# An attention and gated feed-forward kernel on one core: VectorE's order in the second segment, constants, masks and the last tile

## The chip, the core and the metric

The kernel runs on one core of a Trainium2 chip. A core has TensorE (PE in the profile) for matrix products, VectorE (DVE), ScalarE (ACT) and GpSimd (POOL) for elementwise work, SyncE (SP), which here only issues transfers, and 16 DMA engines. PE writes to PSUM; VectorE and ScalarE read it from there. Each engine works through its own instructions in the order in which they stand, and waits at one whose inputs are not ready. The metric is the time of one execution in device microseconds, lower is better; three executions are shown, and one more was taken with the profiler.

## The reference

With B=4 batches, H=8 heads, S=768 positions, D=64, 4 sink positions and a window of 128:

```python
scores = scale * np.matmul(q, k.transpose(0, 1, 3, 2))
keep = is_sink | in_window              # k < 4, or 0 <= q - k < 128
scores = np.where(keep, scores, -1000000000.0)
a = np.exp(scores - max)
a = a / (np.sum(a, axis=-1, keepdims=True) + 1e-09)
x = np.matmul(a, v)                     # heads side by side: 3072 x 512
H = np.maximum(x @ w_h, 0.0)
T = 1.0 / (1.0 + np.exp(-(x @ w_t + b_t)))
out = T * H + (1.0 - T) * x
```

## The kernel before, in words

The 3072 tokens are 24 tiles of 128, six to a batch. A loop over n (L447) is a pipeline by hand: step n computes the scores and the exponential of tile n, the attention values and the division of tile n-1 (n1), and the feed-forward part of tile n-2 (nb). A helper at the end keeps each engine's instructions in the order in which the program writes them, so the order of the code is the order of each engine.

*q and k.* Each is loaded by four transfers per segment, one for each head of a group (load_part, L104); batch 0 has three segments of 256 positions, the others two of 384, called (1,0), (1,1) and so on. Most go through POOL's queue, which turns fp32 into fp16 on the way. Only the first two segments of q of batch 0 come in fp32 through SP (and half of the first through ACT) and are cast on VectorE and ScalarE, half each (cast_q, L423). VectorE then transposes in pieces of four positions per row (transpose_qk, L125): two pieces for a segment of batch 0, three for the others. All the pieces of a segment are needed before the scores that read it.

*Scores and masks.* For a tile, PE adds a mask to PSUM by eight small matmuls of mk and mq (L265; four at the last tile of a batch), then the products of k and q (L272). ScalarE takes the exponential (E, L319), 128x2048. A column of ones beside V gives the row sums. The sink positions go through sink_scores (L285), sink_expo (L293) and the vs tile (L309); vs comes from the sinks' V and a mask vmask, multiplied on POOL (sink_values, L254). sink_scores for batch 1 stands first in step n=8 and reads all of that batch's q, so it needs both its segments.

*Values and the feed-forward part.* values (L330, L333) multiplies E by V; norm (L341, L343, VectorE) divides and gives X. X is transposed on PE (L354) and copied to XT on ScalarE (L359). gate (L363) adds the product with wt to the bias row in ps_z (L303), tanh follows on ScalarE (L370); hidden (L379) puts the product with wh into ps_h, of which there is one. VectorE then makes diff (L386), gate_value (L374, on POOL for tiles 14 to 22), gated (L391); POOL adds X (finish, L397; on VectorE for the last two tiles) and SP stores. I call gate_value, gated and finish of a tile its "complete". diff frees ps_h for the next hidden.

*Order in steps 2 to 7.* hidden_at (L421) says which hidden runs in which step: none in 2, tile 0 in 3, tile 1 in 4, tiles 2 and 3 in 5, then nb. pieces (L408) puts three transposes of segment (1,0) in n=5, one of (1,1) in n=6 and two in n=7, behind norm and the V cast; up to n=7 the completes come after them. cast_v (L142) is on VectorE for tiles 0 to 4, then on POOL. V tiles 2 to 7 are requested on SP behind the scores of tiles 0 to 5.

*The start.* idle (L405) is products of zeros that keep PE busy: 18 before step 0, 8 in it, 6 in step 1. SP issues the first q, the four sink loads (L173), the second q, then V. POOL issues k, the bias, the third segment, wt, wh, makes vmask (L235 to L240, nine operations), vs, and then issues (1,0). A POOL transfer waits until the eighth transfer before it on its queue has landed. VectorE sets constants by memset: ones (L222), the ones columns of eight V tiles and of the sinks (L231, L232).

Of the kernel before, what the change touches and what calls it, by code (L numbers as in the profile page):

```python
# [37 lines left out]
def kernel(  # L38
# [34 lines left out]
    LATER = 14  # L73

# [83 lines left out]
    vmask = const.tile([P, H], FP32, tag="vmask")  # L158
    skmask = const.tile([P, HG, H], FP16, tag="skmask")
# [11 lines left out]
    def load_sinks(b):  # L171
        for g in range(G):
# [5 lines left out]
              allow_small_or_imprecise_dtypes=True)  # L178
    for i in range(2):
        for g in range(G):  # L180
            load_part(0, i, g, 1)
    load_sinks(0)
    for g in range(G):
        load_part(0, 1, g, 0, into=first[1], engine=sp)
    pool.dma_start(out=brow[0:P:32, :], in_=moe_b_t.unsqueeze(0).to_broadcast([G, DM]))
# [3 lines left out]
    pool.dma_start(out=wh, in_=moe_w_h.rearrange("(kc p) of -> p kc of", p=P))  # L189
# [29 lines left out]
    def bias_row():  # L219
        dve.memset(ones, 0.0)  # L220
        for g in range(G):
            dve.memset(ones[32 * g:32 * g + 1, :], 1.0)  # L222

    def ones_columns():
        dve.memset(skmask, 0.0)
        for g in range(G):
            for hg in range(HG):
                h = hg * G + g
                dve.memset(skmask[32 * g:32 * g + 32, hg, h:h + 1], 1.0)
        for tile_v in vt:  # L230
            dve.memset(tile_v[:, :, D:D + 1], 1.0)  # L231
        dve.memset(vs32[:, :, D:D + 1], 1.0)  # L232

    def sink_masks():
        pool.memset(vmask, 1.0)  # L235
        for g in range(G):
            m = vmask[32 * g:32 * g + 32, :]
            pool.affine_select(out=m, in_=m, compare_op=ALU.is_ge, fill=0.0, base=0,
                               pattern=[[-NSINK, H]], channel_multiplier=1)
            pool.affine_select(out=m, in_=m, compare_op=ALU.is_ge, fill=0.0,  # L240
                               base=NSINK - 1, pattern=[[NSINK, H]], channel_multiplier=-1)

# [15 lines left out]
    def scores(n):  # L258
# [3 lines left out]
        for x in range(nq):  # L262
# [5 lines left out]
        for hg in range(HG):  # L268
            for e in range(2):
                for g in range(G):  # L270
# [4 lines left out]
                                     start=False, stop=(e == 1), skip_group_check=True)  # L275
# [39 lines left out]
    def expo(n):  # L315
# [4 lines left out]
                       func=AF.Exp, bias=ebias, scale=SCALE)  # L320

# [55 lines left out]
    def hidden(n):  # L377
        for kc in range(KC):
            pe.matmul(ps_h, lhsT=XT[n][:, kc * P:(kc + 1) * P], rhs=wh[:, kc, :],  # L379
                      start=(kc == 0), stop=(kc == KC - 1))  # L380
# [3 lines left out]
    def diff(n):  # L384
        DD[n] = work.tile([P, DM], FP16, tag="DD", name="DD")
        dve.scalar_tensor_tensor(out=DD[n], in0=ps_h, scalar=0.0,  # L386
                                 in1=X[n].rearrange("p hg g d -> p (hg g d)"),
                                 op0=ALU.max, op1=ALU.subtract)

    def gated(n):  # L390
        dve.tensor_tensor(out=DD[n], in0=DD[n], in1=TH[n], op=ALU.mult)  # L391

    def finish(n):

        o = work.tile([P, DM], FP32, tag="O", name="O")
        eng = dve if n >= N - 2 else pool
        eng.tensor_tensor(out=o, in0=DD[n], in1=X[n].rearrange("p hg g d -> p (hg g d)"),  # L397
                          op=ALU.add)
        sp.dma_start(out=out[n * P:(n + 1) * P, :], in_=o)


# [7 lines left out]
    for n, what in zip([5, 5, 5, 6, 7, 7, 9, 10, 11, 12, 13, 13, 15, 16, 17, 18, 19, 19],  # L409
                       [(b, i, piece) for b in range(1, B) for i in range(2) for piece in range(3)]):  # L410
# [9 lines left out]

    hidden_at = {2: [], 3: [0], 4: [1], 5: [2, 3]}  # L421

    def cast_q(i):  # L423
        dve.tensor_copy(out=nat[0][i][:, 0, 0], in_=first[i][:, 0, 0])
        act.copy(out=nat[0][i][:, 0, 1], in_=first[i][:, 0, 1])

    load_v(0)
    load_v(1)
    cast_q(0)
    transpose_qk(0, 0, 0)  # L430
    transpose_qk(0, 0, 1)
    ones_columns()
    cast_q(1)
# [4 lines left out]
    bias_row()  # L438
    sink_masks()
    sink_values(0)  # L440
    load_segment(1, 0)
    sinks_at = {2: (0, (2, 3)), 4: (0, (4, 5))}
    for b in range(1, B):
        sinks_at[b * NC + 2] = (b, (2, 3, 4, 5))

    idle(18)
    for n in range(N + 2):  # L447

        nb, n1 = n - 2, n - 1
        late = n >= N  # L450
        early = n < 8
        if nb >= 0 and not late:
# [6 lines left out]
        if n < N:  # L459
# [5 lines left out]
            if n % NC == 3 and n // NC + 1 < B:  # L465
                load_sinks(n // NC + 1)
        starts(n1 if 0 <= n1 < N else None, nb if nb >= 0 else None)
        old = hidden_at.get(n - 1, [n - 3])[-1:]
        new = hidden_at.get(n, [nb] if nb >= 0 else [])
        if nb >= 1:  # L470
            for m in old:
                diff(m)
# [4 lines left out]
        if not early:  # L477
            for piece in pieces.get(n, ()):
                transpose_qk(*piece)
        if n == 0:  # L480
            idle(8)
        if 0 <= n1 < N:
            values(n1)
            norm(n1)
        if 0 < n < LATE:
            cast_v(n, dve)
        if n == 1:
            idle(6)
        if early:
            turn = pieces.get(n, ())  # L490
            for piece in turn[:1]:
                transpose_qk(*piece)
            for m in new[:-1]:
                hidden(m)
                diff(m)
            for piece in turn[1:]:
                transpose_qk(*piece)
        if nb >= 1:
            for m in old + new[:-1]:
                if m < LATER:  # L500
                    gate_value(m)
                gated(m)
                finish(m)
        if nb >= 0:
# [5 lines left out]
            for m in new[-1:]:  # L510
                hidden(m)
# [4 lines left out]
        if n < N and n > NC and n % NC == 1:  # L516
            sink_values(n // NC)
    gate_value(N - 1)
    diff(N - 1)
    gated(N - 1)  # L520
# [36 lines left out]
```

## Time and profile before

| | us |
|---|---|
| three executions | 116.92, 118.16, 118.45 (median 118.16) |
| the profiled execution | 116.57 |
| its span, first to last instruction | 114.9 |
| busy: PE, DVE, ACT, POOL | 101.2, 83.6, 74.5, 86.0 |
| mean granted clock of TensorE | 0.975 |

The page divides the span into 40 slices and gives, for each engine, the busy tenths. "Chain that ended last" is followed back from the last instruction, each time to what released it. In a timeline a line has the start, the time taken, engine, line of the program, operation and tiles, and in brackets the idle time before it with what ended it. A DMA issue is listed with the time from its start to the landing. Busy time of PE is modelled and overlaps from one matmul to the next.

### The profile page before, as it was taken

To read this page: it belongs to the slowest core of one execution; us is meant where nothing else is said; L and a number is where in the kernel's file an instruction comes from. 1 tells how busy PE (TensorE), PEld (TensorE's weight loads), DVE (VectorE), ACT (ScalarE), POOL (GpSimd) and SP (SyncE) were. 2 spreads that over 40 slices of the span, in tenths; PEclk is the share of its full clock that TensorE was granted. 3 is DMA by queue.
4 is the path that set the end of the run, shared out by engine and by line. 5 is a ranking of instruction groups with operands and counts; after the bars stand their busy time and mean duration, and the time that the engine had idled before them with its cause. 6 is when DMAs were issued, how large, how long until landed. Compare 5 with 4: busy or idle time off the path is not lost.

```text
span 114.9 us, 3575 instructions
## 1 busy us (share of the span) xinstructions
PE 101.2 (88%) x1416; PEld 55.3 (48%) x1416; DVE 83.6 (73%) x186; ACT 74.5 (65%) x81; POOL 86.0 (75%) x143
## 2 busy tenths in 40 slices
PE   5998299999968896999999999999999999989910
PEld 2333145555535434656555565655655665544400
DVE  6772977463699997799988959898889446646570
ACT  3401766969724793997758978896678987862400
POOL 6998379859773899999997989948755986555600
PEclk9999859999999999999999999999999999999995
DMA  2999999999999399999999999997766201222222
GB/s 79 207 189 231 216 207 194 226 213 233 218 238 196 128 210 271 256 209 261 214 206 234 279 212 257 200 162 195 208 169 178 102 31 66 91 97 91 87 96 94
DMA packets 35921, 20.82 MB, mean 181 GB/s; under 512 B 27196, under 2 KB 32320, under 8 KB 35904
## 3 DMA queue, kind: packets, MB, share of 16 engines
q1 hardware_dynamic: 29536, 13.50, 44.4%
q0 software_dynamic: 6208, 6.82, 37.6%
q10 hardware_dynamic: 160, 0.26, 0.8%
q8 instruction: 11, 0.18, 0.7%
q14 instruction: 6, 0.05, 0.2%
HBM read 21.11 MB, written 6.29 MB: 239 GB/s over the span
## 4 chain that ended last, share of the span: by engine, by line
PE 46%; DVE 17%; DMA 16%; POOL 11%; issue 4%; ACT 2%; POOLq 1%; DVEq 0%; ACTq 0%
DMA nat<-in_k_dram 11%; PE ps_z L363 11%; PE ps_h L379 10%; DVE tr L125 7%; POOL nat L108 6%; PE ps_s L272 5%; DMA nat<-in_q_dram 5%; PE ps_av L330 5%; PE ps_av L333 4%; PE ps_s L265 3%; PE ps_av L354 3%; DVE X L343 3%; DVE DD L386 3%; PE ps_z L303 2%; DVE DD L391 2%
## 5 line engine op out<-in xcount | busy, mean ns | idle before, releaser
L319 ACT ACTIVATE E<-ps_s,ebias 128x2048 f16<-128x2048 f32 (+1 forms) x24 | 43.8, 1826 | 5.1 <-PE ps_s L272 4.8
L397 POOL TENSOR_TENSOR O<-DD,X 128x512 f32<-128x512 f16 x22 | 25.5, 1159 | 15.6 <-DVE DD L391 12.5
L379 PE MATMUL ps_h<-wh,XT 128*128 128x512 f16 x96 | 24.6, 379 | 1.3 <-DVE DD L386 1.3
L125 DVE STREAM_TRANSPOSE tr<-nat 128x512 f32<-128x512 f32 x24 | 24.9, 1081 | 1.0 <-DMA nat<-in_k_dram 0.8
L363 PE MATMUL ps_z<-wt,XT 128*128 128x512 f16 x96 | 24.6, 379 | 0.2 <-DMA wt<-in_moe_w_t_dram 0.2
L108 POOL DMA_DIRECT2D nat<-in_k_dram x36 | 19.7, 554 | 2.3 <-DMA nat<-in_k_dram 1.1
L386 DVE SCALAR_TENSOR_TENSOR DD<-ps_h,X 128x512 f16<-128x512 f32 x24 | 16.5, 687 | 4.5 <-PE ps_h L379 3.6
L370 ACT ACTIVATE TH<-ps_z 128x512 f16<-128x512 f32 x24 | 14.2, 592 | 7.9 <-PE ps_z L363 7.8
L359 ACT COPY XT<-ps_av 128x512 f16<-128x512 f16 x24 | 14.0, 584 | 7.8 <-PE ps_av L354 6.2
L343 DVE TENSOR_TENSOR X<-ps_av,rec 128x512 f16<-128x512 f32 x24 | 16.6, 692 | 0.9
L341 DVE RECIPROCAL rec<-ps_av 128x8 f32<-128x8 f32 x24 | 4.9, 202 | 16.3 <-PE ps_av L333 15.0
L108 POOL DMA_DIRECT2D nat<-in_q_dram x28 | 15.7, 559 | 1.1 <-DMA nat<-in_k_dram 0.5
L379 PEld LDWEIGHTS <-XT 128*128 128x128 f16 x96 | 9.2, 98 | 12.2 <-issue 1.8
L272 PE MATMUL ps_s<-tr 32*128 32x256 f16 (+1 forms) x384 | 14.5, 267 | 0.6 <-DVE tr L125 0.3
L333 PE MATMUL ps_av<-v,E 128*128 128x65 f16 x192 | 14.3, 196 | 0.0
L330 PE MATMUL ps_av<-v,E 128*128 128x65 f16 x160 | 12.5, 194 | 0.0
L333 PEld LDWEIGHTS <-E 128*128 128x128 f16 x192 | 11.8, 99 | 1.4 <-ACT XT L359 1.0
L330 PEld LDWEIGHTS <-E 128*128 128x128 f16 x160 | 10.1, 97 | 4.7 <-issue 4.7
L391 DVE TENSOR_TENSOR DD<-DD,TH 128x512 f16<-128x512 f16 x24 | 11.5, 480 | 0.7
L405 PE MATMUL ps_h<-zeros 128*128 128x512 f16 x32 | 10.7, 502 | 1.3 <-DVE zeros L175 1.3
L265 PE MATMUL ps_s<-mq,mk 32*128 32x256 bf16 x176 | 9.3, 279 | 2.7 <-ACT E L319 2.7
L142 POOL CAST v<-V 128x512 f16<-128x512 f32 x19 | 11.7, 615 | 0.0
(58 smaller groups left out, 100.5 us busy)
## 6 DMA issues: line engine op xcount, KB each, us to landing
V<-in_v_dram SPq DMA_DIRECT2D x24, 256.0 KB, 6.2
out_dram<-O SPq DMA_DIRECT2D x24, 256.0 KB, 3.3
nat<-in_q_dram POOLq DMA_DIRECT2D x24, 96.0 KB, 5.7
nat<-in_k_dram POOLq DMA_DIRECT2D x24, 96.0 KB, 5.5
first<-in_q_dram SPq DMA_DIRECT2D x6, 128.0 KB, 3.9
nat<-in_k_dram POOLq DMA_DIRECT2D x12, 64.0 KB, 4.3
wt<-in_moe_w_t_dram POOLq DMA_DIRECT2D x1, 512.0 KB, 7.3
wh<-in_moe_w_h_dram POOLq DMA_DIRECT2D x1, 512.0 KB, 8.6
```

The source lines that it names most:

```text
L108: engine.dma_start(out=into[32 * g:32 * g + 32, which].rearrange("p hg m d -> p hg (m d)"), in_=(q, k)[which][b, :, t0:t0 + nt, :].rearran ...
L125: dve.transpose(out=dst[:, :, 4 * piece:4 * piece + 4, :], in_=src)
L272: last = pe.matmul(ps_s[:, g, hg, 0:nq * P], lhsT=tr[b][rows, 1, hg, c * P:(c + 1) * P, e], rhs=tr[b][rows, 0, hg, c * P:(c + nq) * P, e], ...
L319: act.activation(out=E[n][:, :, :, 0:nq * P], in_=ps_s[:, :, :, 0:nq * P], func=AF.Exp, bias=ebias, scale=SCALE)
L330: pe.matmul(slot, lhsT=E[n - 1][:, g, hg, P:2 * P], rhs=v_of(n - 1)[:, h, :], start=first, stop=False, skip_group_check=True)
L333: pe.matmul(slot, lhsT=E[n][:, g, hg, 0:P], rhs=v_of(n)[:, h, :], start=first, stop=True, skip_group_check=True)
L343: dve.tensor_tensor(out=X[n], in0=av[:, :, :, 0:D], in1=rec.unsqueeze(3).to_broadcast([P, HG, G, D]), op=ALU.mult)
L363: pe.matmul(ps_z, lhsT=XT[n][:, kc * P:(kc + 1) * P], rhs=wt[:, kc, :], start=False, stop=(kc == KC - 1), skip_group_check=True)
L370: act.activation(out=TH[n], in_=ps_z, func=AF.Tanh, scale=0.5)
L379: pe.matmul(ps_h, lhsT=XT[n][:, kc * P:(kc + 1) * P], rhs=wh[:, kc, :], start=(kc == 0), stop=(kc == KC - 1))
L386: dve.scalar_tensor_tensor(out=DD[n], in0=ps_h, scalar=0.0, in1=X[n].rearrange("p hg g d -> p (hg g d)"), op0=ALU.max, op1=ALU.subtract)
L397: eng.tensor_tensor(out=o, in0=DD[n], in1=X[n].rearrange("p hg g d -> p (hg g d)"), op=ALU.add)
```

## The change

It has five parts.

1. The second segment of q of batch 0 is issued on SP straight behind the first; V of tiles 0 and 1 next, the sink loads last. Its cast is done by VectorE alone, 128x1024.
2. The rows of ones, the ones columns of V and of the sinks are written by 13 small ScalarE activations (Copy with bias 1). vmask starts from an iota on POOL and is finished by five small VectorE operations behind the cast of V tile 0. On POOL vs now stands ahead of wh and of segment (1,0).
3. VectorE's order in steps 4 to 8 is written out (turns). The transposes of batch 1 are spread over steps 4 to 7. In steps 0 to 3, norm comes ahead of them as before, but in step 1 the third segment's transposes now come ahead of the cast of V tile 1. idle in step 1 goes from 6 to 4.
4. For tiles 20 to 23 no mask is added on PE; VectorE multiplies E by wmask (0 or 1, made on POOL in step 15) ahead of values.
5. The last tile's hidden, diff, gated, finish and store go in two halves of 256 columns, the left finish on POOL. Tile 22's finish moves to POOL.

```diff
+    DVE_MASK = N - 4
     for i in range(2):
         for g in range(G):
             load_part(0, i, g, 1)
-    load_sinks(0)
     for g in range(G):
         load_part(0, 1, g, 0, into=first[1], engine=sp)
+    load_v(0)
+    load_v(1)
+    load_sinks(0)
...
         for tile_v in vt:
-            dve.memset(tile_v[:, :, D:D + 1], 1.0)
+            act.activation(out=tile_v[:, :, D:D + 1], in_=zeros[:, 0:H].unsqueeze(2),
+                           func=AF.Copy, bias=1.0)
...
+    def windows():
+        pool.memset(wmask, 1.0)
+        pool.affine_select(out=wmask[:, 0], in_=wmask[:, 0], compare_op=ALU.is_ge, fill=0.0,
+                           base=0, pattern=[[1, P]], channel_multiplier=-1)
...
+    def mask(n):
+        nq = 2 if n % NC + 1 < NC else 1
+        e = E[n].rearrange("p g hg (x q) -> p (g hg) x q", x=2)[:, :, 0:nq]
+        dve.tensor_tensor(out=e, in0=e, in1=wmask[:, 0:nq].unsqueeze(1)
+                          .to_broadcast([P, H, nq, P]), op=ALU.mult)
...
-    hidden_at = {2: [], 3: [0], 4: [1], 5: [2, 3]}
+    def complete(m):
+        if m < LATER:
+            gate_value(m)
+        gated(m)
+        finish(m)
+    turns = {4: [(diff, 0), (norm, 3), (transpose_qk, 1, 0, 0), (complete, 0)],
+             5: [(diff, 1), (transpose_qk, 1, 0, 1), (norm, 4), (hidden, 2), (diff, 2),
+                 (transpose_qk, 1, 0, 2), (complete, 1)],
+             6: [(diff, 3), (norm, 5), (transpose_qk, 1, 1, 0), (complete, 2)],
+             7: [(diff, 4), (transpose_qk, 1, 1, 1), (norm, 6), (transpose_qk, 1, 1, 2),
+                 (complete, 3)],
+             8: [(diff, 5), (norm, 7), (complete, 4), (complete, 5)]}
+    last_hidden = {2: (), 3: (0,), 4: (1,), 5: (3,)}
+    sink_values(0)
+    pool.dma_start(out=wh, in_=moe_w_h.rearrange("(kc p) of -> p kc of", p=P))
+    load_segment(1, 0)
...
+        if DVE_MASK <= n1 < N:
+            mask(n1)
         starts(n1 if 0 <= n1 < N else None, nb if nb >= 0 else None)
...
-            idle(6)
+            idle(4)
...
+    left, right = slice(0, DM // 2), slice(DM // 2, DM)
     gate_value(N - 1)
-    diff(N - 1)
-    gated(N - 1)
-    finish(N - 1)
+    diff(N - 1, left)
+    gated(N - 1, left)
+    finish(N - 1, left)
+    diff(N - 1, right)
+    gated(N - 1, right)
+    finish(N - 1, right, dve)
```

137 lines of the change are left out of this document (70 added, 67 removed).

## The prediction, made before the changed kernel had run

> **What bounds the kernel now.** I read the slices of the page, then the chain that ended last, then the timelines of the engines, where brackets hold the idle time before an instruction and its releaser.
>
> ```profile
> PE   5998299999968896999999999999999999989910
> DVE  6772977463699997799988959898889446646570
> ...
> PEclk9999859999999999999999999999999999999995
> DMA  2999999999999399999999999997766201222222
> ...
> PE 46%; DVE 17%; DMA 16%; POOL 11%; issue 4%; ACT 2%; POOLq 1%; DVEq 0%; ACTq 0%
> ```
>
> A slice is 2.87 us. TensorE is full from about 48 us to 105; there a tile takes 3.65 us (transposes of X at 51.79 and 55.43 in the PE timeline). Before that it has holes, with VectorE at 9 in the twelfth to fifteenth slice (31.6 to 43 us). The DMA engines are full from 2.9 us. The chain agrees: POOL and DMA to 32 us, VectorE to 44, PE to about 103, VectorE at the end. So three stretches can give something: the front, the PE-bound stretch, the tail. The front, on VectorE and TensorE:
>
> ```profile
> 28.06 0.69 DVE L343 TENSOR_TENSOR X<-ps_av,rec 128x512 f16<-128x512 f32 x1
> ...
> 31.41 0.21 DVE L341 RECIPROCAL rec<-ps_av 128x8 f32<-128x8 f32 x1 [1.07 <-ACT E L319]
> ...
> 36.55 1.28 DVE L391 TENSOR_TENSOR DD<-DD,TH 128x512 f16<-128x512 f16 x1
> ...
> 42.21 1.97 DVE L125 STREAM_TRANSPOSE tr<-nat 128x512 f32<-128x512 f32 x2
> ```
>
> ```profile
> 44.23 0.43 PE L285 MATMUL ps_av<-tr,sk 128*32 128x64 f16 x31 [0.83 <-DVE tr L125]
> ```
>
> From the end of X for tile 3 (28.75) VectorE works, idle once for 1.07, to 44.18, and the sink scores of n=8 wait for its last transpose. It is VectorE's order and not a late load that holds this: by the DMA issues, segment (1,0)'s last part was issued at 23.33 and took 5.5 (landed 28.8), (1,1)'s at 29.09 and took 5.2 (34.3), while their first transposes start at 32.26 and 39.19.
>
> The clock, in a table of 1 us stretches (PE, PEld, DVE, ACT, POOL busy with counts, PEclk, DMA share, GB/s), and the tail:
>
> ```profile
> 12.00:13.00 1.00, 0.00 (x0) 0.00 (x0) 1.00 (x2) 1.00 (x1) 0.24 (x1) 1.00 1.30 212
> ...
> 14.00:15.00 1.00, 1.00 (x24) 0.60 (x16) 0.79 (x6) 0.00 (x0) 0.55 (x1) 0.50 1.34 233
> ```
>
> ```profile
> 109.38 0.29 DVE L374 TENSOR_SCALAR TH<-TH 128x512 f16<-128x512 f16 x1
> 109.59 0.68 DVE L386 SCALAR_TENSOR_TENSOR DD<-ps_h,X 128x512 f16<-128x512 f32 x1
> 110.31 0.42 DVE L391 TENSOR_TENSOR DD<-DD,TH 128x512 f16<-128x512 f16 x1
> 110.77 0.69 DVE L397 TENSOR_TENSOR O<-DD,X 128x512 f32<-128x512 f16 x1
> ```
>
> PE waits 2.8 us (10.95 to 13.73) for E of tile 0, which waits on ScalarE behind the cast of the second q; then the clock is 0.50 for 3.3 us. At the end 2.1 us of VectorE and 3.4 us of store (111.46 to 114.9) follow the last tanh.
>
> **The front, step by step.** *Loads.* On SP the four sink loads (1.70 to 4.71) no longer stand ahead of the second q: it is issued from 1.70 instead of 4.75, V of tiles 0 and 1 somewhat earlier, the sinks behind them, needed only by vs. On POOL the nine vmask operations go (15.19 to 17.39); one iota comes (0.23, as away's), and vs now waits for VectorE's masks, at about 14 to 15, with wh and segment (1,0) queued behind it: wh at about 16 instead of 14.45, (1,0) from about 17 instead of 18.48. That buys and costs nearly nothing: landings on POOL's queue were 17.1 (last third-segment part, 11.23 + 5.9), 20.1 (wt, 12.76 + 7.3), 23.05 (wh, 14.45 + 8.6), 28.8, 34.3: in order, spaced by size (3 us per 512 KB, 5.5 to 5.8 per 768 KB) and not by issue, so the queue is always full. wh is late only if issued after wt has landed. What helps is the DMA share of 0.50 in the first 4 us, partly filled by the earlier q: everything behind lands 0 to 1.0 us earlier, or 0.5 later (V of tiles 3 and 4 is asked for earlier, as its scores are). I take 0.4 earlier.
>
> *ScalarE.* Its cast of the second q (0.62, after 5.38 of waiting) goes, so E of tile 0 starts after its scores (9.2) and not at 11.72. Thirteen small activations come: at most 0.36 each (es, 64x128), at least 0.06 (the memsets that they replace), at 0.2 done by 8.4, at 0.36 by 10.5. They lie beside the wait for the transposes: nothing; if that cover goes, 1.3 at most, still under the old 11.72.
>
> *VectorE.* Nine memsets of 0.065 and four of 0.165 go (1.2); half a cast more (0.27), the mask's five small operations between 0.06 (memset) and 0.23 (away) each come, 0.7 in all: equal within 0.3, behind loads. But third-segment transposes now stand before the cast of V tile 1: they wait for 17.1 less 0.4 and end at 18.7, the cast at 19.1 (before 17.08), values of tile 1 at 19.15 (before 19.26). So n=2 gains nothing: wt's gate at 19.7 (20.11), n=3 at 20.7 (21.02), n=4 at 24.6 (24.94): 0.3.
>
> *The five steps.* Before, X(3) to the last transpose is 15.4 us, with six transposes, three norms, diffs 1 to 4 and completes 0 to 3 in it. After, complete(3) stands behind the last transpose (0.65 out of the chain), and gated(2), 1.28 instead of 0.42 at 36.55 because POOL had started O(1) at 36.40, no longer follows complete(1) directly (0.86). Completes 4 and 5 now stand together, so gated(5) may stretch in the same way, beside PE work of n=8. Bottom-up: six transposes of 0.95, three norms of 0.9, four diffs of 0.62, three completes of 0.65, a V cast of 0.37 are 13.2; waits for values of tiles 4 and 5, about 1.0. That is 14.2, against 15.4: 1.2. The first transpose now wants (1,0) at 28.4, its landing (28.8 less 0.4): no stall, but no slack; each us later is a us in the chain, and the V cast of tile 4 and diff(1) queue behind it, for which values(4) and hidden(2) wait. (1,1) lands at 34, wanted at 37.
>
> Front: 0.3 + 1.2 + 0.1 (idle 6 to 4, hidden) = 1.6 earlier at n=8; bounds 2.3 earlier (landings 1.0 earlier) and 0.3 later (first rival). From n=8 on PE is the bound with unchanged work to n=19.
>
> **The masks.** Removed: 28 PE mask matmuls, 0.33 per eight in the chain, 0.12 for four: 1.1. Added: three multiplications of 128x2048 f16 and one of 128x1024. The f16 TENSOR_TENSOR rows are 0.194 at 64 elements and 0.42 at 512: 0.51 ns each, so 1.2 and 0.7 us. Upper bound by the f32 row (0.691 at 512): 2.4. VectorE then has 1.2 + 0.62 + 0.9 + 0.42 = 3.15 per tile, under PE's 3.32. values(n1) waits for the mask and diff queues behind it. E is ready in time: E(20) at 92.0, gated(17) ends at 92.44. POOL builds wmask at n=15 (about 0.9 by ident's two rows of 0.29), beside 1.84 of idle before 77.86; without that it would be 0.9 on the V casts. Whether VectorE and POOL run freely is doubtful:
>
> ```profile
> 91.77 0.67 DVE L391 TENSOR_TENSOR DD<-DD,TH 128x512 f16<-128x512 f16 x1
> ```
>
> ```profile
> 91.54 0.61 POOL L142 CAST v<-V 128x512 f16<-128x512 f32 x1
> ```
>
> This gated took 0.67 and ended 0.29 after POOL's cast; so did those at 36.55 and 47.91. The other 21 took about 0.42. Bounds: 1.3 gained (1.1 and its share behind norm), 0.4 lost (second rival). As most rows are free, I take 0.8 gained.
>
> **The last tile.** GV 0.29, two diffs of 0.42, two gated of 0.29, one O of 0.42 make 2.1, as before: halves add an overhead each. finish(22) moves to POOL, but gate_value waited for tanh (109.35) anyway: nothing. Left: the last store is half as large. Of its 3.4 us between nothing and 0.7 goes (256 KB at the 200 GB/s of the front are 1.3); against it the right gated may meet POOL's left O, 0.3. I take 0.4 gained.
>
> Sum: 1.6 + 0.8 + 0.4 = 2.8. The profiled execution took 116.57 (span 114.9 and 1.7 around it): 113.8. The runs were 116.92, 118.16, 118.45; the median of all four is 117.54, so I state **114.7**.
>
> **Rivals.** *The clock halves in n=2* (17%). Scores(2) end at 16.3 to 17.2, values(1) start at 19.15: a hole of 1.9 to 2.8 us. A hole of 2.8 halved the clock for 3.3 us; holes up to 0.9 did not. Then 1.6 us of work doubles in n=2 and 3, n=8 is 0.3 late: 117.54 + 0.3 - 0.8 - 0.4 = 116.6. The Trainium skill, "TensorE: Matmul & The Clock Gate", section "What's actually happening", says that the clock falls after an idle window of about 3.4 us; by that, the clock would stay and the sum hold, but this trace fell after 2.8.
>
> *POOL and VectorE take turns* (18%). If each mask and gated excludes POOL's O (1.15), gate value (0.6) and cast (0.6), a tile takes 2.35 + 0.3 + 1.2 = 3.85 instead of 3.65; three tiles lose 0.6, the first 0.33 stays, the right gated loses 0.3: 117.54 - 1.6 + 0.3 - 0.1 = 116.1. For it: the three rows above; against it: the other 21. The Trainium skill, "SBUF — State Buffer", section "SBUF: two separate sides", states it as a rule: a VectorE operation with two SBUF inputs and a GpSimd operation lock a shared port for the whole instruction, whichever starts first; it speaks against the masks, and the three rows agree.
>
> *Masks at one element per 1.1 ns* (8%), by the f32 row, because wmask is broadcast over heads: 2.4 + 2.65 = 5.05 per tile, 1.4 more on three, 0.7 on the last: 4.6 lost, 117.54 - 1.6 + 4.6 - 0.4 = 120.1, slower than before. It decides from masks of 1.7 us on (3 x (1.7 + 2.65 - 3.65) = 2.1, the rest of the gain). Against it: the two inner dimensions are contiguous.
>
> **Numbers.** Forecast 50%, rivals 17, 18, 8, and 7% that loads land earlier still and the masks are free: 116.57 - 2.3 - 1.3 - 0.7 = 112.3. The range 112.3 to 117.3 reaches past both middle rivals (a run as high as 118.16 adds 0.6) and leaves out the third and the edges. Two per cent is about what a measurement of this kernel tells from no change: 115.8 and 120.5. Faster: 47 of the forecast's 50, the 7, 6 of the middle rivals: 60%. Slower: 8 and 1. Within: 31.
>
> **What would show it.** The first L285 of n=8 near 42.6; idle on VectorE before the first transpose of segment (1,0) means a late load; PEclk 0.5 near 20 us the first rival. Mask rows near 1.2 us and tile steps of 3.3 to 3.5 from n=20 on the forecast; mask or gated rows longer beside POOL rows the second. The prediction is wrong if wh's landing stops hidden(0) or steps from n=9 to 19 are not 3.65.

## The result, and the profile after

The kernel after takes 123.69 us (median of 122.28, 123.53, 123.85 and 124.34), the kernel before beside it 117.72: a ratio of 1.047, 95% interval 1.034 to 1.060. It is slower; 114.7 was forecast. A run over 1.5% above its kernel's fastest is left out of the ratios: here the 124.34, all but one of `sinks_first`, which so has no ratio, 8 of 12 of `early_q` (118.8 to 119.8) and 5 of 12 of `order_vector_end`, whose profile, like that of `sinks_first`, is of such a run. The profiled execution took 122.28 with a span of 120.6, against 116.57 and 114.9: 5.7 us more.

The slices and the shares of the chain, on the page of the kernel after (a slice is 3.0 us):

```profile
PE   5942998999389979969999999999999999899100
...
DVE  6708967352597995999898958987794988874800
...
PEclk9999599999999999999999999999999999999855
DMA  3999999999979699999999999867843122122220
...
PE 41%; DMA 22%; DVE 17%; POOL 8%; issue 3%; ACT 3%; DVEq 0%; ACTq 0%; POOLq 0%
```

Three places to look at: PE has a 3 in the eleventh slice (30.2 to 33.2 us) and a 6 in the eighteenth (51.3 to 54.3), where before had a 9 in the slices of the same number; the chain has 22% DMA, where it had 16%; and PE and VectorE are empty in the last two slices, when the arithmetic is over and the kernel still runs. The front in VectorE's timeline, with the idle time before each instruction in brackets:

```profile
28.47 0.69 DVE L366 TENSOR_TENSOR X<-ps_av,rec 128x512 f16<-128x512 f32 x1
31.37 1.06 DVE L126 STREAM_TRANSPOSE tr<-nat 128x512 f32<-128x512 f32 x1 [2.20 <-DMA nat<-in_q_dram]
...
37.46 0.42 DVE L420 TENSOR_TENSOR DD<-DD,TH 128x512 f16<-128x512 f16 x1
...
44.18 1.06 DVE L126 STREAM_TRANSPOSE tr<-nat 128x512 f32<-128x512 f32 x1
```

gated(2) takes 0.42 as forecast (1.28 before), but the first transpose of (1,0) starts only when the load has landed, after 2.20 of idling. Steps n=8 to n=10 on PE, then the stretch of VectorE and GpSimd that holds n=10 (each line has its engine):

```profile
45.29 0.43 PE L302 MATMUL ps_av<-tr,sk 128*32 128x64 f16 x31 [0.79 <-DVE tr L126]
...
54.14 0.40 PE L377 MATMUL ps_av<-ident,X 128*128 128x128 f16 x4 [0.73 <-DVE X L366]
```

```profile
48.92 0.42 DVE L420 TENSOR_TENSOR DD<-DD,TH 128x512 f16<-128x512 f16 x1
...
49.58 2.15 DVE L420 TENSOR_TENSOR DD<-DD,TH 128x512 f16<-128x512 f16 x1
...
50.27 1.16 POOL L426 TENSOR_TENSOR O<-DD,X 128x512 f32<-128x512 f16 x1
```

The first DVE line is gated(4), the second gated(5), which took 2.15. At the end, GpSimd's and VectorE's last operations (the span ends at 120.6):

```profile
113.18 0.67 POOL L426 TENSOR_TENSOR O<-DD,X 128x256 f32<-128x256 f16 x1 [0.94 <-POOL O L426]
...
114.03 0.42 DVE L426 TENSOR_TENSOR O<-DD,X 128x256 f32<-128x256 f16 x1
```

The transposes of X of tile 8 (n=10) and of tile 23 on PE, in the kernel before, and of tile 23 in the kernel after:

```profile
51.79 0.39 PE L354 MATMUL ps_av<-ident,X 128*128 128x128 f16 x4
...
106.11 0.40 PE L354 MATMUL ps_av<-ident,X 128*128 128x128 f16 x4 [0.23 <-DVE X L343]
```

```profile
108.45 0.40 PE L377 MATMUL ps_av<-ident,X 128*128 128x128 f16 x4 [0.23 <-DVE X L366]
```

Milestones, from these lines and those of before, say where the 5.7 us went:

| stretch | before | after | lost |
|---|---|---|---|
| start to n=8 (its sink scores) | 44.23 | 45.29 | 1.06 |
| n=8 to n=10 (X transposes) | 7.56 | 8.85 | 1.29 |
| n=10 to X transposes of tile 23 | 54.32 | 54.31 | 0 |
| from there to the end of the last O | 5.35 | 6.00 | 0.65 |
| last O to the end of the span | 3.44 | 6.15 | 2.71 |

The masks on VectorE lie in the third stretch, and changed nothing.

### The profile page after: what moved, and what is told of

The parts are those of the page before. It is cut to its first block, busy times and chain, and to the rows that moved or that the text cites. A ratio compares the mean times of both kernels' runs of the same rounds, so it can differ in the third digit from the quotient of the medians.

```text
span 120.6 us, 3527 instructions
## 1 busy us (share of the span) xinstructions
PE 100.2 (83%) x1390; PEld 54.7 (45%) x1390; DVE 87.5 (73%) x183; ACT 76.2 (63%) x93; POOL 90.1 (75%) x140
## 4 chain that ended last, share of the span: by engine, by line
PE 41%; DMA 22%; DVE 17%; POOL 8%; issue 3%; ACT 3%; DVEq 0%; ACTq 0%; POOLq 0%
PE ps_z L386 9%; PE ps_h L402 9%; DMA nat<-in_k_dram 8%; DMA nat<-in_q_dram 8%; DVE tr L126 7%; DMA wh<-in_moe_w_h_dram 6%; POOL nat L109 5%; PE ps_av L353 4%; DVE X L366 4%; PE ps_s L288 4%; PE ps_av L377 4%; PE ps_av L356 3%; DVE DD L415 2%; PE ps_s L281 2%; PE ps_z L320 2%
## 5 line engine op out<-in xcount | busy, mean ns | idle before, releaser
L426 POOL TENSOR_TENSOR O<-DD,X 128x512 f32<-128x512 f16 (+1 forms) x24 | 30.4, 1269 | 13.2 <-DVE DD L420 8.8
L402 PE MATMUL ps_h<-wh,XT 128*128 128x512 f16 (+1 forms) x100 | 24.6, 370 | 0.7 <-DVE DD L415 0.7
L393 ACT ACTIVATE TH<-ps_z 128x512 f16<-128x512 f32 x24 | 14.2, 593 | 10.8 <-PE ps_z L386 10.8
L415 DVE SCALAR_TENSOR_TENSOR DD<-ps_h,X 128x512 f16<-128x512 f32 (+1 forms) x25 | 16.6, 664 | 3.3 <-PE ps_h L402 2.7
L402 PEld LDWEIGHTS <-XT 128*128 128x128 f16 x100 | 9.7, 97 | 11.8 <-issue 1.5
L364 DVE RECIPROCAL rec<-ps_av 128x8 f32<-128x8 f32 x24 | 4.7, 197 | 13.9 <-PE ps_av L356 13.9
L420 DVE TENSOR_TENSOR DD<-DD,TH 128x512 f16<-128x512 f16 (+1 forms) x25 | 12.9, 515 | 0.7
L288 PEld LDWEIGHTS <-tr 32*128 32x128 f16 x384 | 9.2, 93 | 5.3 <-DVE tr L126 4.2
L432 PE MATMUL ps_h<-zeros 128*128 128x512 f16 x30 | 10.0, 500 | 1.3 <-DVE zeros L178 1.3
```

The costliest lines, as they stand in the source:

```text
L288: last = pe.matmul(ps_s[:, g, hg, 0:nq * P], lhsT=tr[b][rows, 1, hg, c * P:(c + 1) * P, e], rhs=tr[b][rows, 0, hg, c * P:(c + nq) * P, e], ...
L393: act.activation(out=TH[n], in_=ps_z, func=AF.Tanh, scale=0.5)
L402: pe.matmul(ps_h[:, cols], lhsT=XT[n][:, kc * P:(kc + 1) * P], rhs=wh[:, kc, cols], start=(kc == 0), stop=(kc == KC - 1), skip_group_check ...
L415: dve.scalar_tensor_tensor(out=DD[n][:, cols], in0=ps_h[:, cols] if h is None else h, scalar=0.0, in1=flat(X[n], cols), op0=ALU.max, op1=A ...
L426: eng.tensor_tensor(out=O[n][:, cols], in0=DD[n][:, cols], in1=flat(X[n], cols), op=ALU.add)
```

## The experiments

Each was timed beside the kernel before. In the table, "n=8" is the start of those of its sink scores that wait for VectorE's last transpose (31 of 32), "to n=10" from there to the X transposes of n=10, "end" from the X transposes of tile 23 to the end of the span, each from one profile; "landing" is the issue of the eighth part of (1,0) plus its time to landing, good to 0.1 us. The last two kernels load and use only half of the weights and so compute something else; they stand for the timing alone.

| run | ratio (95%) | landing | n=8 | to n=10 | end |
|---|---|---|---|---|---|
| before | 1 | 28.8 | 44.23 | 7.56 | 8.79 |
| after | 1.047 (1.034-1.060) | 31.1 | 45.29 | 8.85 | 12.15 |
| whole_tile | 1.042 (1.035-1.049) | 32.5 | 47.59 | 8.84 | 10.47 |
| sinks_first | none | 30.8 | 45.86 | 8.84 | 12.09 |
| completes_apart | 1.044 (1.038-1.051) | 30.4 | 44.44 | 8.01 | 12.15 |
| pe_masks | 1.050 (1.042-1.057) | 31.2 | 45.32 | 8.84 | 12.03 |
| wh_first | 1.055 (1.048-1.062) | 31.6 | 45.69 | 8.85 | 12.15 |
| old_loads | 1.041 (1.035-1.048) | 30.3 | 44.42 | 8.86 | 12.11 |
| halves_only | 1.032 (1.023-1.040) | 31.0 | 45.51 | 7.55 | 11.71 |
| order_alone | 1.031 (1.024-1.037) | 30.8 | 44.93 | 8.02 | 10.13 |
| late_copy | 1.027 (1.021-1.032) | 29.4 | 43.98 | 7.55 | 11.96 |
| pool_early | 0.999 (0.994-1.003) | 29.8 | 44.47 | 7.56 | 8.54 |
| halves_vector | 1.003 (0.999-1.006) | 29.2 | 44.07 | 7.55 | 9.16 |
| spread_early | 1.001 (0.997-1.005) | 30.2 | 44.70 | 7.55 | 8.54 |
| vector_end | 1.032 (1.027-1.037) | 31.6 | 45.66 | 8.86 | 8.87 |
| o4_vector | 1.038 (1.032-1.045) | 31.3 | 46.39 | 7.85 | 12.07 |
| early_q | 0.998 (0.994-1.002) | 30.6 | 44.29 | 7.55 | 8.74 |
| order_vector_end | 0.999 (0.994-1.003) | 32.5 | 47.65 | 8.02 | 8.30 |
| order_half_weights | 0.987 (0.983-0.991) | 27.1 | 42.45 | 8.02 | 8.29 |
| before_half_weights | 0.991 (0.988-0.995) | 28.0 | 43.07 | 7.55 | 8.77 |

### The end

Theory first: the halves lengthen the end. Rival: something else does.

```diff
-            if n == N + 1:
-                for cols in (slice(0, DM // 2), slice(DM // 2, DM)):
-                    hidden(nb, cols)
...
-    diff(N - 1, left)
...
-    finish(N - 1, right, dve)
+    diff(N - 1)
+    gated(N - 1)
+    finish(N - 1, eng=dve)
```

> The kernel after, with only the last tile whole again (one hidden, one diff, one gated, one O on VectorE, one store of 256 KB). Theory: the halves are what makes the end long. Then the time from the last O to the end of the span is about 3.4 us as before the change, not 6.15, and the last O ends 0 to 0.6 earlier; the time falls by 2.7 to 3.3 us, to a ratio of 1.020 to 1.025 against the kernel before. Rival: the long end has nothing to do with the halves; then about 6 us stay after the last O, and the ratio is 1.042 or more.

The end fell from 12.15 to 10.47, and 4.75 stayed after the last O, where before has 3.44. So the theory had half of it: the halves are not all. The ratio stayed at 1.042, the rival's value: in this profile n=8 came at 47.59, 2.3 us later than in the kernel after, which is more than the 1.7 that the end gave back. The same from the other side, the kernel before with halves:

> The kernel before, with only the last tile in halves (two hidden, two diffs, two gated, the left O on GpSimd and the right on VectorE, two stores of 128 KB; O of the tile ahead of it on GpSimd too). Theory: the halves lengthen the end: from the last O to the end of the span 6.1 us instead of 3.44, and the last O about 0.3 to 0.6 later; 2.5 to 3.3 us slower, ratio 1.021 to 1.028. Rival, by the kernel after with a whole last tile (4.75 us after the last O, 0.5% faster): 1.3 to 1.7 us, ratio 1.011 to 1.015. Forecast's own step: 0.4 faster, 0.997.

The end became 11.71, 2.9 longer, and the ratio 1.032, above the range; in this profile n=8 was 1.3 later too. Laid side by side, the ten profiles had one thing in common: the span ended 6.3 to 6.75 us after GpSimd's last operation. In before this is the gate value of tile 22 (it ended at 108.20, the span at 114.9: 6.7), in after the left half of the last O (113.85 and 120.6: 6.75), in whole_tile O of tile 22 (114.52 and 121.2: 6.7). New theory: GpSimd takes that long to close, whatever it did last. The line of GpSimd's timeline in the kernel before that this rests on:

```profile
107.58 0.62 POOL L374 TENSOR_SCALAR TH<-TH 128x512 f16<-128x512 f16 x1
```

The next two kernels test it from both sides, on the kernel before.

```diff
-    finish(N - 1)
+    o = finish(N - 1)
+    pool.tensor_copy(out=scrap, in_=o[:, 0:1])
```

> The kernel before, with one added operation: a GpSimd copy of one column of the last O into a tile that nobody reads, behind that O. In the ten profiles so far the span ends 6.3 to 6.75 us after GpSimd's last operation, whatever that is, while the last O ends 3.4 to 6.2 us before the end. Theory: GpSimd needs 6.3 to 6.75 us after its last operation, and this sets the end. Then the copy at about 111.6 puts the end at 118.1 to 118.4 where the last O is at 111.46, 6.7 to 7.0 us after that O; the time rises by 3.2 to 3.6 us, to a ratio of 1.027 to 1.031. Rival: the long end comes from the stores (two halves, or O of tile 22 from GpSimd); then 3.4 us stay after the last O and the ratio is 1.000 within 0.004.

```diff
-        eng = dve if n >= N - 2 else pool
+        eng = dve if n >= N - 3 else pool
-        eng = pool if LATER <= n < N - 1 else dve
+        eng = pool if LATER <= n < N - 2 else dve
```

> The kernel before, with O of tile 21 and the gate value of tile 22 on VectorE instead of GpSimd, so that GpSimd ends with the gate value of tile 21, about 105. Theory as for the added copy: GpSimd's close then ends at about 111.6, and the last store sets the end: its data were moved at about 113.5 in the kernel before, so the span ends 2.1 to 2.5 us after the last O instead of 3.44, and the time falls by 0.9 to 1.3 us, to 0.989 to 0.992. VectorE was idle 1.5 us where the two operations go (they cost 0.69 and 0.29). Rival: the store needs 3.4 us; ratio 1.000 to 1.004.

The last operations of late_copy (span 117.8), and of pool_early (span 114.9):

```profile
110.51 0.69 DVE L397 TENSOR_TENSOR O<-DD,X 128x512 f32<-128x512 f16 x1
...
111.26 0.19 POOL L524 COPY scrap<-O 128x1 f32<-128x1 f32 x1 [3.32 <-DVE O L397]
```

```profile
104.56 0.62 POOL L374 TENSOR_SCALAR TH<-TH 128x512 f16<-128x512 f16 x1
...
111.02 0.69 DVE L397 TENSOR_TENSOR O<-DD,X 128x512 f32<-128x512 f16 x1
```

A copy of 0.19 us that nobody reads put the end at 117.8, 6.35 after it and 6.6 after the last O: 2.65% for one column. The theory holds for the loss. With GpSimd done at 105.2, its close would end at 111.9; the span ended at 114.9, 3.19 after the last O (111.71), so the store and what follows it take 3.2 us and not the 2.1 to 2.5 that I expected. In the kernel before the two ends, 6.7 after GpSimd and 3.4 after the last O, coincided.

The traces also show what the close is. Behind its last operation GpSimd has an instruction DRAIN, which the timelines leave out. The list of what belongs to one line of the program has it, here for before, after and pool_early (count; shortest, median and longest in ns; first and last start in us):

```profile
L552 POOLq DRAIN  x3: 46/102/7160, 106.6 to 114.6; - x3
```

```profile
L590 POOLq DRAIN  x3: 46/154/6260, 113.2 to 120.3; - x3
```

```profile
L552 POOLq DRAIN  x3: 46/102/7158, 103.6 to 114.6; - x3
```

The longest of each is the first. In before it starts at 106.61 and ends at 113.77, 5.57 us after GpSimd's last operation, and in all twenty profiles it ends 5.56 or 5.57 after it; where it ends last, 0.8 to 1.15 us with semaphore instructions follow. In pool_early it was over at 110.75, before the last O. Why a DRAIN takes that long, no run here shows.

The halves without GpSimd, and the kernel after without GpSimd at its end:

> The last, with the last tile in halves as in the kernel after, but every O from tile 21 on on VectorE. Theory: halves cost nothing by themselves, and the 3.7 us that they cost with GpSimd in them (ratio 1.0317) were GpSimd's late end; the ratio is within 0.004 of the run without halves. Rival 1, the forecast's step: halves gain 0.4 us, 0.985 to 0.988. Rival 2: two small stores are slow by themselves; 1.01 or more.

> The kernel after, with GpSimd out of the end: O of tiles 21, 22 and of the left half of 23, and the gate value of 22, on VectorE. Theory (the span ends 6.4 to 6.7 us after GpSimd's last operation, or 3.2 after the last O, whichever is later): 3.2 us after the last O, the transposes of X of tile 23 to the end 8.8 us as before the change, instead of 12.15; 3.0 to 3.4 us faster than the kernel after, ratio 1.018 to 1.024. Rival: VectorE, which has the masks too, is late with the operations it takes over; the last O comes 1 us later and the ratio is 1.03.

Halves that stay on VectorE are worth nothing either way (1.003; the last O came 5.80 after the transposes of tile 23 against 5.35, and the smaller last store left 3.36 after it, where before has 3.44). In the kernel after, the end fell from 12.15 to 8.87, as expected. The ratio fell by 1.5 points, less than the 2.3 to 2.9 expected, to the value that the rival had; but the rival's mechanism isn't there (the last O is 5.80 after the transposes, 6.00 in the kernel after), and the two intervals leave room for 2.3.

### The masks

```diff
-    DVE_MASK = N - 4
+    DVE_MASK = N
...
-        if n == 15:
-            windows()
```

> The kernel after, with all masks added on TensorE again, and without the three operations that build the window mask. Theory: the last masks on VectorE save TensorE about 0.2 us a tile, which VectorE's and GpSimd's mutual waits take back; the time moves by less than 0.4 us (ratio 1.044 to 1.050). Rival 1: the forecast's gain of 0.8 us is there and hidden by other losses; then this kernel is 0.8 us slower than the kernel after, 1.054. Rival 2: the masks cost more than they save; then it is 0.5 us faster or more, 1.042 or lower.

Nothing moved: 54.31 us from n=10 to tile 23 with masks on VectorE, 54.31 on PE; the ratio, 1.050, lies in the range expected. Why shows on PE and ScalarE in one tile, first in the kernel after (no masks on PE), then with them:

```profile
94.72 0.39 PE L377 MATMUL ps_av<-ident,X 128*128 128x128 f16 x4
95.03 0.63 PE L288 MATMUL ps_s<-tr 32*128 32x256 f16 x16
95.51 0.37 PE L320 MATMUL ps_z<-brow,ones 32*128 32x512 f16 x1
95.82 0.39 PE L326 MATMUL ps_av<-vs,es 32*128 32x260 f16 x2
```

```profile
95.18 0.58 ACT L382 COPY XT<-ps_av 128x512 f16<-128x512 f16 x1 [0.37 <-PE ps_av L377]
```

```profile
94.74 0.39 PE L377 MATMUL ps_av<-ident,X 128*128 128x128 f16 x4
95.06 0.40 PE L281 MATMUL ps_s<-mq,mk 32*128 32x256 bf16 x8
95.28 0.62 PE L288 MATMUL ps_s<-tr 32*128 32x256 f16 x16
95.75 0.37 PE L320 MATMUL ps_z<-brow,ones 32*128 32x512 f16 x1
95.84 0.39 PE L326 MATMUL ps_av<-vs,es 32*128 32x260 f16 x2
```

```profile
95.20 0.59 ACT L382 COPY XT<-ps_av 128x512 f16<-128x512 f16 x1 [0.26 <-ACT TH L393]
```

L326 writes ps_av, which also holds the transposed X, and so follows ScalarE's copy of it, which ended at 95.77 without the masks and at 95.79 with them. It starts at 95.82 without the masks and at 95.84 with them: the loop transposes, copy, values sets the tile, and scores and masks lie beside the copy. The masks themselves took 1.21 us, as forecast. O on GpSimd took 2.06 or 2.07 beside each of the three whole ones instead of 1.15, and nobody waited for it:

```profile
94.70 1.21 DVE L342 TENSOR_TENSOR E<-E,wmask 128x2048 f16<-128x2048 f16 x1
```

```profile
94.86 2.07 POOL L426 TENSOR_TENSOR O<-DD,X 128x512 f32<-128x512 f16 x1 [0.36 <-DVE DD L420]
```

### The completes of n=8

```diff
-             8: [(diff, 5), (norm, 7), (complete, 4), (complete, 5)]}
+             8: [(diff, 5), (complete, 4), (norm, 7), (complete, 5)]}
```

> The kernel after, with complete(4) put ahead of the norm of tile 7 in the fifth step, so that complete(5) no longer follows it directly. Theory: gated(5) took 2.15 us because GpSimd's O(4) ran beside it, and this cost 1.3 us between n=8 and n=10. Then gated(5) takes 0.4 to 0.7, n=10 starts 6.9 us after n=8 (as before the change, 7.6) or up to 7.6, instead of 8.85, and the ratio is about 1.036. Rival: what is late there is the load of the next segment or GpSimd itself; then the n=8 to n=10 stretch stays at 8.5 us or more, and the ratio at 1.045 to 1.05.

The stretch to n=10 fell from 8.85 to 8.01, two thirds of the loss of 1.29, and the ratio was 1.044, where about 1.036 was expected. gated(5) took 0.43, but beside GpSimd's work the two gate values took 0.87 and 1.23 and gated(4) 1.16. Then O of tile 4 alone was taken from GpSimd:

```diff
-    finish(m)
+    finish(m, eng=dve if m == 4 else pool)
```

> The kernel after, with only O of tile 4 on VectorE instead of GpSimd. Theory: gated(5) waits for GpSimd's O(4); then gated(5) takes 0.42 instead of 2.15, VectorE spends 0.69 on O(4), and n=8 to n=10 falls from 8.85 to 7.6 to 8.0 us; ratio 0.7 to 1.0% lower than the kernel after, 1.037 to 1.040. Rival: GpSimd's loads stretch it, or the chain is on another engine; gated(5) stays over 1.5 us or the stretch at 8.5 or more, ratio 1.045 to 1.05.

```profile
50.01 0.42 DVE L420 TENSOR_TENSOR DD<-DD,TH 128x512 f16<-128x512 f16 x1
50.47 0.69 DVE L426 TENSOR_TENSOR O<-DD,X 128x512 f32<-128x512 f16 x1
...
51.40 0.42 DVE L420 TENSOR_TENSOR DD<-DD,TH 128x512 f16<-128x512 f16 x1
```

In VectorE's timeline gated(5) is 0.42 again, and n=10 comes 7.85 after n=8 with 0.69 more work on VectorE: GpSimd's O(4) is what gated(5) waited for. The forecast's second rival put this in the masks, where it happened and cost nothing; here the stretch is 1.29 longer than before, and freeing gated(5) gave back 0.84 and 1.00 of it. The Trainium skill, "SBUF — State Buffer", section "SBUF: two separate sides", says that the later of the two instructions is held for the whole of the other; here gated(5) began 0.7 us ahead of O(4) by the record and still ended 0.3 after it, so this trace shows the exclusion but not which came first.

In the kernel before, gated(2) is stretched the same way (1.28). Taking that out gave nothing:

```diff
+            if new[:-1]:
+                for m in old:
+                    gate_value(m)
+                    gated(m)
+                    finish(m)
             for piece in turn[1:]:
                 transpose_qk(*piece)
```

> The run with GpSimd ending early, and in step n=5 complete(1) put ahead of the last two transposes, so that complete(2) doesn't follow it directly. Theory: a gated that follows another complete waits for GpSimd's O (gated(2) took 1.28 in the kernel before, 2.08 in the run with halves alone, 2.15 for gated(5) in the kernel after, 0.42 else); then gated(2) takes 0.42, n=8 starts 0.9 to 1.6 us earlier relative to the first transpose of segment (1,0) (before: 12.0 us, 12.8 with 2.08), that is 11.1 to 11.2, and the ratio is 0.977 to 0.983. Rival: the time moves into the next load or into gated(1); ratio as without it.

gated(2) took 0.42, yet n=8 came 11.92 us after the first transpose of (1,0), against 11.97 in the kernel before. In its place VectorE waited 0.43 and 0.19 for PE's values. What a stretched instruction costs has to be read from the next wait.

### The loads and the written order

The theories: the early q delays the first keys and with them all else; or wh, put behind vs, does.

```diff
+    load_sinks(0)
     for g in range(G):
         load_part(0, 1, g, 0, into=first[1], engine=sp)
...
     pool.dma_start(out=wt, in_=moe_w_t.rearrange("(kc p) of -> p kc of", p=P))
+    pool.dma_start(out=wh, in_=moe_w_h.rearrange("(kc p) of -> p kc of", p=P))
```

The first line alone is sinks_first, the second wh_first, both are old_loads.

> The kernel after, with only SyncE's queue as it was: the four sink loads ahead of the second segment's q. Theory: the early q takes the DMA engines from the first keys. Then the first transpose of the keys starts 2.5 us earlier and scores of tile 0 at about 8.6 instead of 11.28, segment (1,0) lands at about 29 instead of 31.4, and the sink scores of n=8 start at 44.2 or earlier, instead of 45.29; the ratio is 1.038 or lower. Rival: the keys are late for another reason (the iota, the order on GpSimd); then scores of tile 0 stay at about 11.3 and the ratio within 0.005 of 1.047.

> The kernel after, with only wh's load put back ahead of vs on GpSimd's queue (behind wt, as before the change). The run with the sinks first showed the first keys early (transposes from 6.96) and yet n=8 as late as 45.86, so the early q is not what holds n=8. Theory: wh, issued at 16.64 behind the wait of vs for the mask, lands late, the eighth part of segment (1,0) waits for it, and the DMA queue runs low meanwhile. Then wh is issued at about 14.8 and lands at 22.5 to 23.2, segment (1,0) lands at 29 to 30, n=8 starts at 43 to 44 instead of 45.29, and the ratio is about 1.035. Rival: the DMA engines were full anyhow, the bytes decide, and (1,0) lands at 31 as with wh late; n=8 stays at 45 or more, the ratio at 1.045.

> The kernel after, with both orders of loads as before: the sinks ahead of the second q on SyncE, wh ahead of vs on GpSimd. Theory that both matter: (1,0) lands at 28.8 as before, and n=8 starts at 42.7 (28.8 plus the 13.9 us from the landing to n=8 in the kernel after), the ratio is about 1.025. If only wh matters: as the run with wh alone, within 0.4 us at n=8. Rival, by which VectorE's written order is the loss and not the loads: n=8 at 45 with (1,0) landed at 29.

In VectorE's timeline of sinks_first the keys are early, and the second q late instead:

```profile
6.96 2.03 DVE L126 STREAM_TRANSPOSE tr<-nat 128x512 f32<-128x512 f32 x2 [0.67 <-DMA nat<-in_k_dram]
11.23 0.69 DVE L453 CAST nat<-first 128x1024 f16<-128x1024 f32 x1 [2.24 <-DMA first<-in_q_dram]
```

(In the kernel after the two stand at 9.21 and 11.07.) n=8 did not gain. Nor did wh alone bring anything (1.055): it was issued at 14.13 instead of 16.64, yet the eighth part of (1,0), which waits for its landing, went at 25.31 (24.65 in the kernel after). Both theories fell as single causes; both orders together gave 44.42 and 1.041, which the intervals don't separate from the kernel after. The early q alone in the kernel before:

> The kernel before, with only the order of the loads on SyncE changed: the second segment's q and V of tiles 0 and 1 ahead of the four sink loads. Theory: the first keys land 2 to 2.5 us later (VectorE's first transpose at about 9 instead of 7), the rest of the loads up to 1 us later, and n=8 starts at 44.7 to 45.5 instead of 44.0 to 44.7 (five profiles with the loads of before); ratio 1.004 to 1.010. Rival 1, the forecast's step: landings 0.4 earlier, ratio 0.997. Rival 2: nothing comes through, as PE waits in n=1 anyway; 1.000 within 0.003.

In its profile the keys came later (first transpose at 8.95, before 6.45), and n=8 stayed at 44.29 though (1,0) landed at 30.6: the old order didn't notice. That is the pattern of the whole table. In the seven profiles with the old order and full weights (1,0) landed at 28.8 to 31.0, and its first transpose started at 32.0 to 32.8. In the eleven with the written order it landed at 30.3 to 32.5, and the transpose started 0.1 to 0.3 after. What the written order is worth was then tried with the other losses taken out:

> The kernel after with both load orders of before, completes 4 and 5 apart, a whole last tile and all masks on TensorE: what is left of the change is VectorE's order in five steps, the second q's cast on VectorE, and the constants on ScalarE and the sinks' mask on VectorE. Theory: the losses of the kernel after are in the loads, the adjacent completes and the last tile; without them the written order gives its gain: n=8 at about 42.7, n=10 at 50.2 to 50.6, the last O 1 us earlier than before the change, and the ratio is 0.990. Rival: the written order itself costs: ratio 1.01 or more.

> The kernel after with the loads in the order of before, the completes 4 and 5 apart, the last tile whole, all masks on TensorE, and GpSimd out of the end; what is left is VectorE's order in five steps, the second q's cast on VectorE, the constants on ScalarE and the sinks' mask on VectorE. Its twin with GpSimd in the end was at 1.0308 (1.0244 to 1.0373). Theory: the end gives 1.3 us back, the rest is 0.45 between n=8 and n=10 and about 0.4 at n=8, so the ratio is 1.007 to 1.015 and the written order gains nothing. Rival 1: the order has its gain and a bad landing hid it; ratio 0.995 or lower. Rival 2: the order itself costs; 1.02 or more.

order_alone still had O of tile 22 on GpSimd and so a long end. Without it the ratio is 0.999, below the range that I gave, so the order neither gains nor costs by this measure. The end explains only part of the step from 1.031: it became 1.83 us shorter, 1.6 points of 3.2, and the rest is open. Last, landings as early as the forecast had assumed:

```diff
-    pool.dma_start(out=wh, in_=moe_w_h.rearrange("(kc p) of -> p kc of", p=P))
+    pool.dma_start(out=wh, in_=moe_w_h[0:DM // 2].rearrange("(kc p) of -> p kc of", p=P))
...
-            pe.matmul(ps_h[:, cols], lhsT=XT[n][:, kc * P:(kc + 1) * P], rhs=wh[:, kc, cols],
+            pe.matmul(ps_h[:, cols], lhsT=XT[n][:, kc * P:(kc + 1) * P], rhs=wh[:, kc % (KC // 2), cols],
```

> The kernel with VectorE's written order, loads of before, no halves, no masks on VectorE and GpSimd out of the end (ratio 0.9987), with only the first half of wt and wh loaded (256 KB each instead of 512) and used for both halves of the contraction, so that the gate and the hidden layer are computed from half of the weights; instructions are as many as before. Theory: n=8 comes 13.9 to 14.2 us after the landing of segment (1,0), which 512 KB less on GpSimd's queue brings to about 28; then n=8 is at 42.0 to 42.8, the forecast's 42.6, and the ratio to the kernel before is 0.980 to 0.988. Rival: V of tiles 3 and 4 or the values hold the chain instead; n=8 stays at 43.7 or later.

> The kernel before with the same half loads of wt and wh. Theory: its first transpose of segment (1,0) waits for VectorE's order and not for the landing, so it starts at 31.5 to 32.3 though (1,0) lands at about 26 to 28, n=8 stays at 43.5 to 44.2, and the ratio is 0.993 to 1.000. Rival: the loads hold the old order as well (V of tile 3); then n=8 falls to 42.8 or less as in the other, ratio 0.985 or lower.

The first transpose of (1,0) on VectorE and the sink scores of n=8 on PE, in the written order, then in the old one:

```profile
27.91 0.69 DVE L367 TENSOR_TENSOR X<-ps_av,rec 128x512 f16<-128x512 f32 x1
28.52 1.07 DVE L126 STREAM_TRANSPOSE tr<-nat 128x512 f32<-128x512 f32 x1
```

```profile
42.45 0.42 PE L303 MATMUL ps_av<-tr,sk 128*32 128x64 f16 x31 [0.79 <-DVE tr L126]
```

```profile
26.89 0.69 DVE L343 TENSOR_TENSOR X<-ps_av,rec 128x512 f16<-128x512 f32 x1
...
31.09 1.07 DVE L125 STREAM_TRANSPOSE tr<-nat 128x512 f32<-128x512 f32 x1
```

```profile
43.07 0.42 PE L285 MATMUL ps_av<-tr,sk 128*32 128x64 f16 x31 [0.85 <-DVE tr L125]
```

With the load there, X(3) to n=8 takes 14.54 in the written order and 16.18 in the old: 1.6 us less, more than the forecast's 1.2, and n=8 came at 42.45 where 42.6 was forecast. But X(3) itself came 1.02 later, as X(1) already had (20.33 against 19.25), and n=10 another 0.47, so of 1.6 little is left (spans of 113.1 and 113.7; 0.987 against 0.991, intervals overlapping). I had expected the old order to stay untouched, and it did not quite: its first transpose came at 31.09, with the whole front 1 us earlier.

## Why the prediction was wrong, step by step

- **Loads: the step that failed in the front.** "(1,0) at 28.4, its landing (28.8 less 0.4): no stall, but no slack" took one landing of one profile. It was the earliest of seven in the old order (up to 31.0), and nothing depended on it there. In the kernel after it was 2.3 later and not 0.4 earlier. The early q, priced as a gain of up to 1.0 for everything behind it, took its time from the first keys: their transposes start at 9.21 in the kernel after and at 6.96 with the sinks ahead. "The queue is always full" failed too: between 12 and 18 us GpSimd's queue moved 0.68 MB instead of 0.90, as wt and wh were issued 1.2 and 2.2 later. The chain itself was sized well: 13.9 us from the first transpose to n=8, 14.2 forecast from the end of X(3).
- **The five steps.** The 1.2 us are there (1.6) when the load is. The sentence that gated(5) may stretch beside n=8 was right, but it had no price: 1.29.
- **ScalarE.** The activations are hidden, as forecast: they ended at 8.2. But E of tile 0 started at 12.23, behind the late keys, where 9.2 was forecast and 11.72 was before.
- **VectorE in the start.** The third segment's transposes ahead of V tile 1 gave n=3 at 21.47; 20.7 was forecast, 21.02 was before.
- **Masks.** Size right (1.21 us each), gain 0 instead of 0.8: "PE is the bound" was read off busy shares. The removed work lay beside ScalarE's copy of X.
- **Last tile: the largest error.** "finish(22) moves to POOL ... nothing" and the left half on POOL cost 3.4 us in the profile, where 0.4 was to be gained. 2.7 of it is GpSimd's close, which the profile of before already held (6.7 us from its last operation to the end), and which I never looked for because the store ended at the same time.
- **Rivals.** The clock in n=2 didn't fall in the profiled run, but it did in two others of the written order, wh_first and completes_apart, behind waits for wt, so the first rival's mechanism exists. The third rival's sum is off: 1.4 on three tiles and 0.7 on the last are 4.9 and not 4.6. Taking turns is real and hit another place. The slower side was given 9%, for masks that cost too much; the mechanisms that decided, a late load on a chain without slack and an engine's close, weren't among the rivals.

No version that computes the whole result beat the kernel before: the lowest, early_q, pool_early, order_vector_end and spread_early, are at 0.998 to 1.001, with 1 in every interval. What stays open is what sets the landing of (1,0). With both orders of loads restored it was 30.3, 30.8 and 32.5 in three profiles; the first two lie inside the range of the old order, so it isn't shown that the written order itself makes it late.

## What to carry to other kernels

Before a step is put right behind a load, collect the landing from several runs: a transfer with slack in the old order shows an accidental time, and the new order will wait for its latest. For work taken off a busy engine, ask which instruction starts earlier; here it was released by another engine's copy, and nothing was gained. At the end of a kernel, measure from each engine's last instruction to the end of the span, and keep late work off the engine that takes long to close (here GpSimd, with 6.3 to 6.75 us).

## What the runs showed of the hardware

- The span ended 6.3 to 6.75 us after GpSimd's last operation in the profiles where GpSimd worked late, and 2.9 to 3.4 us after the last O (store included) where it ended early. The later of the two was the end. 5.56 or 5.57 us of the former are GpSimd's DRAIN, in all twenty profiles.
- A short hole can halve TensorE's clock, but needn't. In the written order PE waits for a V cast behind the late transpose. In four of the twelve profiles with that order the granted clock then fell to 0.50 for about 3 us (holes of 1.84, 2.22, 2.27 and 2.30 us), and n=8 came 14.8 to 15.0 after the first transpose instead of 13.9; after holes of 1.88, 2.15 and 2.28 it didn't. In n=2 it fell behind waits for wt of 1.34 (completes_apart, line below) and 2.03 (wh_first), and not behind one of 1.44 (whole_tile). In whole_tile, PE's hole and the clock in 1 us stretches (the two figures before the last two are the clock and the DMA share):

```profile
34.78 0.19 PE L356 MATMUL ps_av<-v,E 128*128 128x65 f16 x1 [1.84 <-DVE v L143]
```

```profile
34.00:35.00 1.00, 0.21 (x6) 0.21 (x6) 1.00 (x3) 0.00 (x0) 0.52 (x1) 0.93 0.96 142
35.00:36.00 1.00, 1.00 (x16) 0.72 (x14) 1.00 (x2) 0.00 (x0) 1.00 (x2) 0.50 0.40 68
36.00:37.00 1.00, 1.00 (x4) 0.40 (x3) 0.95 (x3) 0.00 (x0) 1.00 (x3) 0.50 0.48 145
```

PE's wait in n=2 of completes_apart, and the clock behind it:

```profile
20.40 1.87 PE L386 MATMUL ps_z<-wt,XT 128*128 128x512 f16 x4 [1.34 <-DMA wt<-in_moe_w_t_dram]
```

```profile
21.00:22.00 1.00, 1.00 (x3) 0.30 (x2) 0.00 (x0) 0.00 (x0) 0.17 (x1) 0.50 1.14 172
```

The Trainium skill, "TensorE: Matmul & The Clock Gate", section "What's actually happening", says that the clock falls after an idle window of about 3.4 us; here it fell after holes of 1.34 to 2.30, so the measured holes decide.
